# A deadline for background work on TensorE, and measured durations, in a kernel's own list scheduler

## Chip, cores, metric

One core of one Trainium2 chip. The metric is device time in microseconds (us) of one execution. Executions that agree within 1.5% of the fastest count as fast and are compared; the kernel before had one slow one (1389.24 us), which is left out of every ratio.

## The reference

A transformer block on 2048 rows of 640, bf16: layer norm, attention with 32 heads of 20, output projection and residual, layer norm, a gated feed-forward of width 1728, residual.

```python
qkv = x_norm @ wqkv                                    # 2048 x 1920
scores = einsum("bhqd,bhkd->bhqk", q, k) * 20 ** -0.5  # 32 heads of 2048 x 2048
p = softmax(scores); o = einsum("bhqk,bhkd->bhqd", p, v)
h = x + o @ wo
h2 = h + (gelu(norm(h) @ w_gate) * (norm(h) @ w_up)) @ w_down
```

## The kernel before

The queries go through in seven chunks (512, 512, 256, 256, 256, 128, 128 rows), cut into 32 slots. Scores stand in tiles of 128 keys by 512 columns. A *unit* is three or two such tiles: TensorE computes them (QK), ScalarE turns them into exponentials (P) in one instruction of 1536 or 1024 columns. Eight tiles a slot (two in the first) are computed on VectorE instead, by integer arithmetic. TensorE then multiplies P by V (PV). Projections, the feed-forward of the chunk before, and layer norms fill the gaps.

The order of every engine's instructions comes from a list scheduler inside the kernel. It gives each operation a price (`dur`), simulates the engines, and emits what it chose. On the chip each engine runs its list in that order and waits on semaphores, so a wrong price costs nothing by itself; it only leads to another order.

QK is row-tiled, PV column-tiled, all else uses the full array. An exponential waits for two things: its scores (QK), and that the PV which reads the old content of its P tiles is done.

Of the kernel before, what the change touches and what calls it, by code (L numbers as in the profile page):

```python
# [16 lines left out]
DRAIN = {"pe": 0.165, "act": 0.115, "dve": 0.085, "pool": 0.05, "sp": 0.0}  # L17
WARM_WIN, WARM_MIN = 3.4, 0.5
PAD_WIN, PAD_MIN = 3.4, 0.42
PE_AGE = 1.5  # L20

MODE_SWITCH = {"pe": 0.105, "act": 1.28}


class Bank:
# [16 lines left out]
class Sched:  # L42
# [43 lines left out]
    def schedule(self):  # L86
        ops = self.ops
        for o in ops:
            o.nd = len(o.deps)
            for d in o.deps:  # L90
                ops[d].succ.append(o.i)
        free_at = [0.0] * 8
        owner = [None] * 8
        last = [None] * 8
        ready = {e: [] for e in ENGINES}
        future = {e: [] for e in ENGINES}
        free = {e: 0.0 for e in ENGINES}
        mode = {e: None for e in ENGINES}
        for o in ops:
            if o.nd == 0:  # L100
                heapq.heappush(ready[o.eng], (o.prio, o.i))
        events = [0.0]
        done = 0
        order = []
        t = 0.0
        recent = collections.deque()
        live = False
        total = len(ops)
        while done < total:
            assert events, "no operation can start"  # L110
            t = heapq.heappop(events)
            while events and events[0] <= t + 1e-9:
                heapq.heappop(events)
            for e in ENGINES:
                while future[e] and future[e][0][0] <= t + 1e-9:
                    _, p, i = heapq.heappop(future[e])
                    heapq.heappush(ready[e], (p, i))
                if free[e] > t + 1e-9:
                    continue
                skipped = []  # L120
                kept = set()
                chosen = None
                while ready[e]:
                    p, i = heapq.heappop(ready[e])
                    o = ops[i]
                    got = []
                    for bk in o.acq:
                        for b in bk.allowed:
                            if owner[b] is None and free_at[b] <= t + 1e-9 and b not in got and b not in kept:
                                got.append(b)  # L130
                                break
                        else:
                            got = None
                            break
                    if got is None:

                        if p[0] == 0:
                            kept.update(bk.allowed[0] for bk in o.acq)
                        skipped.append((p, i))
                        continue  # L140
                    skipped.append((p, i))
                    if chosen is None:
                        chosen, banks = o, got
                        if e != "pe" or p[0] < 1 or o.mode == mode[e] or t - o.ready > PE_AGE:
                            break
                    elif o.mode == mode[e]:
                        chosen, banks = o, got
                        break
                    if len(skipped) >= 60:
                        break  # L150
                for s in skipped:
                    if chosen is None or s[1] != chosen.i:
                        heapq.heappush(ready[e], s)
                if chosen is not None:
                    for bk, b in zip(chosen.acq, banks):
                        bk.b = b
                        owner[b] = bk
                        if last[b] is not None:
                            chosen.deps = set(chosen.deps)
                            chosen.deps.add(last[b])  # L160
                if chosen is None:
                    if e == "pe" and self.warm is not None:
                        while recent and recent[0][0] < t - WARM_WIN:
                            recent.popleft()
                        b = self.warm_bank
                        free7 = (owner[b] is None and free_at[b] <= t + 1e-9
                                 and all(hasattr(ops[d], "fin") and ops[d].fin + 0.06 <= t for d in self.warm_deps))
                        if sum(x for _, x in recent) < WARM_MIN * WARM_WIN and (free7 or live):
                            o = Op()
                            o.i, o.eng, o.lat = len(ops), "pe", DRAIN["pe"]  # L170
                            o.prio, o.sem, o.tag, o.util = (9, 0), None, "warm", 0.213
                            o.acq, o.rel, o.succ, o.dur = [], [], [], 0.215
                            if live and (mode[e] == "col" or not free7):
                                o.fns, o.mode, o.deps = list(self.pad), "col", set()
                            else:
                                o.fns, o.mode = [self.warm], "full"
                                o.deps = set(self.warm_deps) | ({last[b]} if last[b] is not None else set())
                                last[b] = o.i
                            ops.append(o)
                            chosen = o  # L180
                            total += 1
                    if chosen is None:
                        continue
                o = chosen
                if e == "pe" and self.pad is not None and o.tag and o.tag[0] == "O":
                    while recent and recent[0][0] < t - PAD_WIN:
                        recent.popleft()
                    u = sum(x for _, x in recent) + o.util
                    while u < PAD_MIN * PAD_WIN and o.util < 1.1:
                        o.fns = o.fns + self.pad  # L190
                        o.dur += 0.215
                        o.util += 0.213
                        u += 0.213
                    live = o.i not in self.final
                o.start = t
                if o.util:
                    recent.append((t, o.util))
                if o.mode is not None:
                    if mode[e] not in (None, o.mode):
                        o.dur += MODE_SWITCH[e]  # L200
                    mode[e] = o.mode
                free[e] = t + o.dur
                o.fin = t + o.dur + o.lat
                heapq.heappush(events, free[e])
                for bk in o.rel:
                    b = bk.b
                    owner[b] = None
                    free_at[b] = o.fin + SEM_LAT.get((e, "pe"), SEM_ANY)
                    last[b] = o.i
                    heapq.heappush(events, free_at[b])  # L210
                for s in o.succ:
                    q = ops[s]
                    q.ready = max(q.ready, free[e] if q.eng == e == "pe" else o.fin + SEM_LAT.get((e, q.eng), SEM_ANY))
                    q.nd -= 1
                    if q.nd == 0:
                        heapq.heappush(future[q.eng], (q.ready, q.prio, q.i))
                        heapq.heappush(events, q.ready)
                order.append(o)
                done += 1
        self.order = order  # L220
        self.span = max(o.fin for o in ops)
# [93 lines left out]
P_QK, P_PV, P_PRO, P_EPI, P_LN, P_BG = 0, 1, 1.5, 2, 2.5, 3  # L315


def bass_sequential_preLN__mha_block__glu_gated_geglu__prompt_kernel(
# [12 lines left out]
    with ExitStack() as es:  # L331
# [8 lines left out]


        def c_mm(n, passes=1):
            return 0.001 + passes * n / 2400.0

        def c_act(n):
            return 0.052 + n * 0.000833
# [6 lines left out]
        identf = sb("identf", [128, 128], FP32)  # L353
# [19 lines left out]
        osb = sb("osb", [128, 2, 512], FP32)  # L373
# [75 lines left out]
        def cst(fn, key, n=128):  # L449
# [7 lines left out]
           reads=["zer"], writes=["qf1"])  # L457
        op("act", I("activation", f32(qt_all[:, 2, :, :]), zer[:, 0:2].bitcast(FP32).to_broadcast([128, 2048]), ACT.Copy), 1.8, P_QK,
           reads=["zer"], writes=["qf2"])
# [295 lines left out]
        for c, (q0, nq) in enumerate(CHUNKS):  # L755
            n = 512 // nq
# [11 lines left out]
        i, in_slot = 0, {}  # L768
# [178 lines left out]
        def epilogue(s_, bk):  # L947
# [13 lines left out]
            for tt in range(4):  # L961
                op("pe", lambda eng, tt=tt: eng.transpose(bank(b2)[:, tt * 128:(tt + 1) * 128],
                                                          osb[:, s, tt * 128:(tt + 1) * 128], identf[:]),
                   c_mm(128, 4), P_EPI, mode="full", reads=[("osb", s), "identf"], writes=[key], acq=[b2] if tt == 0 else [],
                   after=tuple(aft) if tt == 0 else ())
            bv = lambda: bank(b2).rearrange("p (t j e) -> p t j e", t=4, j=4)
            rcv = rc[:, s, :].rearrange("p (t j) -> p t j", t=4)
# [220 lines left out]
```

## Time and profile before

| | us |
|---|---|
| time, median of the fast runs | 927 to 929 |
| span of the profile | 925.5 |
| up to the first exponential / from first to last / after the last | 35.7 / 853.7 / 36.1 |
| stalls of ScalarE between exponentials, summed | 12.9 |

A *stall* here is what the distance from one exponential's start to the next exceeds the undisturbed 1.331 us (1536 columns) or 0.904 us (1024). I sort those over 0.06 us into two kinds: if a QK matmul started 0.33 to 0.48 us before the delayed exponential, it waited for scores (*late QK*); if none did, its own scores were ready earlier and it waited for P tiles (*P-slot*). The *tail* is what comes after the last exponential.

### The profile page before, as it was taken

How to read it: one execution, taken by the hardware profiler on the slowest of the kernel's cores; microseconds unless marked ns; L12 is line 12 of the kernel's file. 1: busy time of each engine (PE TensorE's matmuls, PEld its weight loads, DVE VectorE, ACT ScalarE, POOL GpSimd, SP SyncE). 2: the span in 40 equal slices, each digit the busy share in tenths (PEclk: the TensorE clock that was granted, in tenths of full speed). 3: DMA queues.
4: the chain of work that ended last, by engine and by line, in shares of the span. 5: the costliest groups of instructions: out<-in, count | busy, mean ns of one | idle time of the engine just before them, and what ended most of it. 6: DMA issues, size and time to landing. Idle time of an engine off the chain costs nothing.

```text
span 925.5 us, 23154 instructions
## 1 busy us (share of the span) xinstructions
PE 845.3 (91%) x10109; PEld 354.8 (38%) x10109; DVE 810.3 (88%) x1703; ACT 885.7 (96%) x801; POOL 35.1 (4%) x117
## 2 busy tenths in 40 slices
PE   3998999999998998999888999999989999999998
PEld 2432322222232222233233333344444445555667
DVE  8859999999898998888798997989998997998873
ACT  6899999999999999999999999999999999999962
POOL 5000000000001000000001000001000000000100
DMA  7301010322550000001021000010100000110000
GB/s 256 95 18 44 18 55 18 90 60 66 152 180 16 15 1 1 1 15 44 1 31 23 9 2 1 16 30 10 37 16 16 9 23 2 31 32 10 10 17 16
DMA packets 39517, 34.36 MB, mean 37 GB/s; under 512 B 19436, under 2 KB 36936, under 8 KB 39416
## 3 DMA queue, kind: packets, MB, share of 16 engines
q1 hardware_dynamic: 39416, 32.89, 12.7%
q8 instruction: 79, 1.29, 0.6%
q14 instruction: 22, 0.18, 0.1%
HBM read 20.12 MB, written 8.09 MB: 30 GB/s over the span
## 4 chain that ended last, share of the span: by engine, by line
ACT 72%; PE 14%; DVE 11%; issue 1%; POOL 0%; DMA 0%
ACT pts L339 46%; ACT rege L339 25%; PE ps L1039 4%; DVE qt_all L339 3%; PE ps L616 3%; PE ps L852 3%; PE ps L339 3%; DVE rege L339 2%; PE ps L1096 2%; DVE qt_all L812 1%; DVE rege L812 1%; DVE stats L339 1%; ACT L339 1%; DVE rege L1074 1%; PE ps L561 0%
## 5 line engine op out<-in xcount | busy, mean ns | idle before, releaser
L339 ACT ACTIVATE pts<-ps 128x1536 bf16<-128x1536 f32 x480 | 573.1, 1379 | 4.9 <-PE ps L852 3.7
L852 PE MATMUL ps<-qt_all,kt_all 32*128 32x256 bf16 (+2 forms) x3584 | 303.4, 289 | 43.2 <-ACT pts L339 27.5
L339 ACT ACTIVATE rege<-ps 128x1536 bf16<-128x1536 f32 x239 | 300.1, 1381 | 2.1 <-PE ps L339 1.5
L852 PEld LDWEIGHTS ps<-qt_all,kt_all 32*128 32x128 bf16 x3584 | 95.0, 92 | 276.8 <-ACT pts L339 160.8
L339 DVE TENSOR_TENSOR qt_all<-qt_all 128x1024 bf16<-128x1024 bf16 (+1 forms) x240 | 164.0, 683 | 3.4
L1039 PE MATMUL ps<-rege,regw 128*128 128x256 bf16 (+2 forms) x980 | 154.7, 290 | 9.9 <-ACT rege L339 4.2
L339 PE MATMUL ps<-pts,v_all 128*21 128x256 bf16 (+2 forms) x2098 | 138.8, 290 | 0.5 <-DVE rege L339 0.5
L812 DVE TENSOR_SCALAR rege<-ps 128x512 int16<-128x512 f32 x154 | 105.3, 685 | 27.6 <-PE ps L852 26.8
L339 DVE TENSOR_SCALAR qt_all<-qt_all 128x1024 bf16<-128x1024 int16 (+1 forms) x288 | 115.8, 417 | 2.5
L339 PE MATMUL ps<-rege,v_all 128*21 128x256 bf16 (+2 forms) x1294 | 113.3, 292 | 0.1
L1039 PEld LDWEIGHTS ps<-rege,regw 128*128 128x128 bf16 x980 | 72.5, 98 | 67.9 <-issue 28.5
L616 PE MATMUL ps<-regw 128*128 128x512 bf16 (+1 forms) x360 | 86.9, 351 | 1.9 <-DVE v_all L749 0.7
L1096 PE MATMUL ps<-regw,rege 128*128 128x320 bf16 x448 | 79.4, 301 | 1.1 <-DVE rege L1064 0.5
L812 DVE TENSOR_SCALAR qt_all<-ps 128x512 int16<-128x512 f32 x96 | 65.6, 684 | 3.7 <-PE ps L852 2.6
L339 DVE TENSOR_SCALAR rege<-rege 128x1024 int16<-128x1024 int16 (+2 forms) x166 | 67.1, 421 | 1.3
L339 DVE TENSOR_TENSOR rege<-rege 128x1024 bf16<-128x1024 bf16 (+3 forms) x103 | 65.5, 644 | 0.9
L339 PEld LDWEIGHTS ps<-pts,v_all 128*21 128x21 bf16 x2098 | 50.2, 91 | 37.2 <-issue 31.6
L339 PE MATMUL ps<-kt_all,zer 128*32 128x512 bf16 x676 | 56.6, 384 | 0.0
L1096 PEld LDWEIGHTS ps<-regw,rege 128*128 128x128 bf16 x448 | 36.7, 97 | 32.4 <-issue 15.8
L339 PEld LDWEIGHTS ps<-rege,v_all 128*21 128x21 bf16 x1294 | 41.0, 91 | 20.6 <-issue 14.3
L1085 DVE TENSOR_TENSOR rege<-rege,ps 128x512 bf16<-128x512 bf16 (+1 forms) x53 | 35.7, 676 | 12.1 <-PE ps L1039 11.8
L616 PEld LDWEIGHTS ps<-regw 128*128 128x128 bf16 x360 | 28.6, 98 | 45.2 <-issue 21.0
(95 smaller groups left out, 574.3 us busy)
## 6 DMA issues: line engine op xcount, KB each, us to landing
rege<-in_A_x_dram SPq DMA_DIRECT2D x6, 640.0 KB, 5.1
q_rows<-regw SPq DMA_DIRECT2D x20, 128.0 KB, 1.7
out_dram<-rege SPq DMA_DIRECT2D x16, 160.0 KB, 2.1
regw<-in_B_w_gate_dram SPq DMA_DIRECT2D x1, 2160.0 KB, 11.9
regw<-in_B_w_up_dram SPq DMA_DIRECT2D x1, 2160.0 KB, 16.9
regw<-in_B_w_down_dram SPq DMA_DIRECT2D x1, 2080.0 KB, 22.9
kt_all<-k_rows SPq DMA_DIRECT2D x12, 160.0 KB
qt_all<-q_rows SPq DMA_DIRECT2D x12, 160.0 KB
```

The costliest lines, as they stand in the source:

```text
L339: return lambda eng: getattr(eng, method)(*args, **kwargs)
L616: yield op("pe", lambda eng, l=l, r=r, k=k: eng.matmul(bank(bk, n), l, r, start=(k == 0), stop=(k == len(steps) - 1)), c_mm(n), prio, mode ...
L812: d_ops.append(op("dve", lambda eng: eng.tensor_scalar(v[:, 512 * h:512 * h + 512], bank(b), EXP_MUL, -32000.0, ALU.mult, ALU.max), c_dve( ...
L852: return lambda eng: eng.matmul(out()[:, kk * nq:(kk + 1) * nq], kt_all[32 * j:32 * j + 32, g, kt * 128:(kt + 1) * 128], qt_all[32 * j:32 ...
L1039: op("pe", lambda eng, a=a, f=f, fi=fi: eng.matmul(bank(bk)[:, fi * nq:(fi + 1) * nq], w[:, a, F0[f]:F0[f] + 128], hnT[:, a, 128 * tb:128 ...
L1074: cp.append(op("dve", lambda eng, bg=bg, fv=fv, w=w: eng.tensor_copy(fv, bank(bg, w)), c_dve(w), p, reads=[kg], writes=hkeys(k), rel=[bg], ...
L1085: hdone.append(op("dve", lambda eng, bu=bu, fv=fv, w=w: eng.tensor_tensor(fv, fv, bank(bu, w), ALU.mult), c_dve(w), p, reads=[ku] + hkeys( ...
L1096: op("pe", lambda eng, f=f, o=o, hf=hf, bk=bk: eng.matmul(bank(bk, 320), ha_f[:, o:o + 128], wd[:, f, hf * 320:(hf + 1) * 320], start=(f = ...
```

## The change

The intent: TensorE should not start background work, a PV or padding that would still run when the next QK has to start; and the scheduler's prices for TensorE should be the measured ones.

```diff
+QK_LEAD = .45
-MODE_SWITCH = {"pe": 0.105, "act": 1.28}
+MODE_SWITCH = {"pe": .098, "act": 1.28}
+        due = None
...
+                    if e == "pe" and due is not None and o.prio[0] > 0 and t < due < t + o.dur + (MODE_SWITCH[e] if mode[e] not in (None, o.mode) else 0):
+                        skipped.append((p, i))
+                        if len(skipped) >= 60:
+                            break
+                        continue
...
-                    while u < PAD_MIN * PAD_WIN and o.util < 1.1:
+                    room = due - t - MODE_SWITCH[e] if due is not None and due > t else 1e9
+                    while u < PAD_MIN * PAD_WIN and o.util < 1.1 and o.dur + 0.215 < room:
...
+                if e == "act":
+                    due = t + o.dur + (0.905 if o.dur > 1.2 else 1.332) - QK_LEAD if o.mode == "exp" else None
...
-            return 0.001 + passes * n / 2400.0
+            return 0.004 + passes * n / 2400.0
...
-                   c_mm(128, 4), P_EPI, ...      # the epilogue's fp32 transposes
+                   c_mm(128, 2.5), P_EPI, ...
```

I call the first block the *gate*, the second the *cap*, the rest the *prices*.

More of the change, by code (lines that the diff above doesn't have):

```diff
@@ L963, in epilogue @@
                                                           osb[:, s, tt * 128:(tt + 1) * 128], identf[:]),
-                   c_mm(128, 4), P_EPI, mode="full", reads=[("osb", s), "identf"], writes=[key], acq=[b2] if tt == 0 else [],
+                   c_mm(128, 2.5), P_EPI, mode="full", reads=[("osb", s), "identf"], writes=[key], acq=[b2] if tt == 0 else [],
                    after=tuple(aft) if tt == 0 else ())
```

## The prediction

> **What bounds the kernel now.** I read the page's first part, then busy time by stage, ScalarE's waits, the timeline of ScalarE, and at the end the tail. The page's first line and the table by stage (us; the stages are before the first exponential, first to last exponential, after the last):
>
> ```profile
> PE 845.3 (91%) x10109; PEld 354.8 (38%) x10109; DVE 810.3 (88%) x1703; ACT 885.7 (96%) x801; POOL 35.1 (4%) x117
> ```
> ```profile
> 0.00:35.67 35.67, 21.14 (x154) 12.28 (x154) 30.25 (x97) 24.58 (x45) 12.12 (x32) 1.00 0.55 186
> 35.67:889.40 853.73, 793.37 (x9530) 316.93 (x9530) 765.76 (x1573) 850.12 (x743) 23.00 (x85) 1.00 0.12 32
> 889.40:925.50 36.10, 30.74 (x428) 25.56 (x426) 14.34 (x35) 11.02 (x14) 0.00 (x0) 1.00 0.04 15
> ```
>
> In the middle stage ScalarE is busy 850.1 of 853.7 us. TensorE's 793.4 is inflated, since matmuls overlap in the trace. The next question is how much of ScalarE's time is avoidable. Its timeline (start us, us, instruction, count, idle before it):
>
> ```profile
> 42.41 4.67 ACT L339 ACTIVATE pts<-ps 128x1536 bf16<-128x1536 f32 x4
> 46.88 2.46 ACT L339 ACTIVATE rege<-ps 128x1536 bf16<-128x1536 f32 x2
> 49.11 4.74 ACT L339 ACTIVATE pts<-ps 128x1536 bf16<-128x1536 f32 x4
> ...
> 92.84 2.37 ACT L339 ACTIVATE pts<-ps 128x1536 bf16<-128x1536 f32 x2 [0.57 <-PE ps L339]
> ```
>
> From 42.41 to 49.11 six exponentials take 6.70 us, so a pair (1536 columns, then 1024) costs 2.235 us at the bare rate. Start to start, the trace's instructions give 1.331 and 0.904 us as the undisturbed values. I summed over all exponentials what the distance to the next exceeds these by: 12.9 us in all, 10.0 of it in 41 stalls over 0.06 us. No single view prints this sum; busy time hides it because a long record overlaps its neighbour. The middle stage is thus 802.4 bare + 12.9 stalls + 36.9 for five excursions to Gelu with their table loads + 1.6 for the last exponential = 853.8. **12.9 us, 1.4% of the span, is all that a perfect QK service could save in this stage.**
>
> What a stall waits for, from ScalarE's waits (us in total, times, longest):
>
> ```profile
> ACT pts L339 <- PE ps L852: 3.7, 1, 3.7
> ...
> ACT rege L339 <- PE ps L339: 1.5, 1, 1.5
> ...
> ACT pts L339 <- PE ps L339: 0.9, 2, 0.6
> ...
> ACT rege L339 <- PE ps L852: 0.7, 2, 0.4
> ```
>
> The first is the start of the stream, before any exponential. L852 is QK. L339 on ps is PV (or its padding): there an exponential waits not for scores but for the PV that still reads the P slot it will overwrite. The three largest stalls (1.57, 0.86 and 0.50 us, at 144, 93 and 196 us) end together with a long PV at the close of a slot; 2.9 of the 12.9 us. Of the rest nearly all are before a 1536-wide exponential after a 1024-wide one, with QK late by 0.06 to 0.6 us.
>
> The tail of 36.1 us is the other term that can move. Its TensorE is busy 30.7 us, and work of the last-but-one query chunk reaches into it:
>
> ```profile
> 900.49 1.70 ACT L339 ACTIVATE rege<-rege 128x1792 bf16<-128x1792 bf16 x1 [2.86 <-DVE rege L1074]
> 902.21 1.28 ACT L339 ACT_TABLE_LOAD   x1
> ```
>
> 1792 columns are 14 blocks of 128, the Gelu of a whole 128-row chunk; the very last chunk's Gelu is done in pieces on qt_all. So chunk 5's feed-forward is a backlog that TensorE had not finished when the exponentials ended.
>
> **What the Trainium skill says.** "ScalarE: Activation LUTs", What happens when an exp ACTIVATE runs: 0.833 ns per element whatever the function. The trace agrees: (1.331 - 0.904) / 512 = 0.834 ns, so nothing here makes an exponential itself cheaper. "TensorE: Matmul & The Clock Gate", Back-to-back issue gap: N/2.4 + 2.5 ns warm. Medians start to start here are 216, 135.5, 109 and 55.5 ns for N = 512, 320, 256, 128, so N/2.4 plus 2 to 3; the new constant of 4 ns is nearer than the old of 1. "TensorEngine Tiling (Array Packing)", Key Properties: changing the tiling mode drains the engine. A row-tiled QK of 512 columns followed by column-tiled PV takes 315 ns against 216, so 99 ns; the new 98 is right and the old 105 too long. "TensorE: Matmul & The Clock Gate", Part 1: the clock is halved after an idle window of about 3.4 us. Every window of this profile shows clock 1.00, so the padding is enough here; the 1389 us run among the three of the kernel before may be such a throttled one, which its times alone can't show.
>
> **The change, part by part.** The program does the same arithmetic: all this code sits in the list scheduler that fixes each engine's order of instructions. Only the order, and the number of padding matmuls (676 in 169 groups of four) and warming ones (55), can change.
>
> 1. Durations in the scheduler. Mode switch 0.105 to 0.098: I count 1586 switches among row, column and full mode in the trace, so 11.1 us less. Matmul constant 1 to 4 ns: 980 + 520 + 448 + 23 = 1971 matmuls priced so, 5.9 us more. Epilogue transposes from 0.214 to 0.137 us: 128 of them, 9.9 us less. Measured, two of these fp32 transposes start 109 or 164 ns apart, mean 144, so the new price is right. Sum: 15 us less TensorE time in the plan, 1.7% of the 854 us. The hardware doesn't get faster; the plan puts background work a little earlier and denser. I estimate 1 to 2 us from this: fewer mismatches in the middle, somewhat less backlog in the tail.
>
> 2. The gate. At the start t of an exponential, due is set to t + 1.332 + 0.905 - 0.45 = t + 1.787, for both widths. That is the latest start for the QK of the second unit on, which reuses this exponential's banks. But at the start of the next exponential due is overwritten, 0.455 us (after 1536) or 0.882 us (after 1024) before it falls due. So a background operation is stopped only if it starts during the exponential and lasts beyond that. A full-mode matmul takes at most 0.217 + 0.098 = 0.315 us, and is never stopped. An unpadded PV with a switch takes 0.436 + 0.098 = 0.534, and is stopped only in the last 0.08 us of a 1536-wide one; long or padded PVs in the last half microsecond. Laying the rule over the trace before, 11 of 333 column-mode runs would have been held. The gap between the overwrite and the banks' release (0.171 us) is unguarded, although a PV started there delays QK by up to 0.25 us. At 11 holds with 0.1 to 0.3 us each, the gate can save 1 to 3 us; a held PV that is released right after the overwrite can also lose as much. I take 1 us of gain.
>
> 3. The cap on padding. A pad group is 0.215 us and is added only while the PV ends before due. Only 17 of the 343 runs I count have three or more groups; a handful will lose one or two. I take 0 to 1 us.
>
> Sum: 12.9 us of stalls fall to some 10, the tail shrinks by 1, so 929.3 - 4 = 925. It is small because what the gate guards is seldom violated.
>
> **The rivals.** (a) Holding PV back keeps the P slots full longer, and the exponential then waits for PV instead of QK. The three largest stalls already have this form; but PV mostly starts right after a QK, 0.4 us into an exponential, where nothing is held. If it did bite at every slot's close (32 slots, 0.3 us), +10 us: 939. (b) TensorE has too little slack and the gate throws some away: idle gaps ahead of QK push the feed-forward back and lengthen the tail. For it: chunk 5's Gelu already sits in the tail. Against it: 48 us of padding and warming (224 times 0.216) plus roughly 100 us of idle (the start-to-start distances beyond N/2.4, 3 ns and a switch, summed) are still there. It would make 930 to 940. (c) The opposite: the denser plan completes chunk 5 before the stream ends, and its TensorE work (140 matmuls at 55.5 ns and 28 at 135.5, 11.6 us) leaves the tail in part: 915 to 920. (d) Less padding lets the clock fall for a window or more: some microseconds a time; if for good, a time like the 1389 us one. (e) The reordering is chaotic: one changed choice shifts everything after it, and 41 stalls are redrawn. I put this noise at +-5 us, which is more than the intended effect.
>
> **Range and chances.** 925, with 914 to 936 eight times in ten: noise and the tail. Over 2% faster means under 910.7, more than all the stalls plus a third of the tail's excess; 2 in 100. Over 2% slower, above 947.9, takes rival (d), or (a) and (b) together: 6 in 100.
>
> **What would show it.** Counts of QK, PV, projection and feed-forward matmuls the same, pads between 560 and 720. Bare exponentials still 1.331 and 0.904 us, 719 of them. Summed stalls 6 to 14 us. First exponential within 0.5 us of 35.67. Tail 31 to 39 us. Clock 1.00. The prediction is wrong if the stalls fall under 4 us (then the gate does much more than the durations above allow), if the tail moves by over 6 us, or if the granted clock falls.

## More of the kernel before

The parts that matter here:

```python
SIZES = (512, 512, 256, 256, 256, 128, 128); PR, PR2 = 12, 6   # 18 P tiles in a ring
D_PER_SLOT = (8,) * len(SIZES)                                  # tiles a slot for VectorE
P_QK, P_PV, P_PRO, P_EPI, P_LN, P_BG = 0, 1, 1.5, 2, 2.5, 3     # lower goes first
...
def schedule(self):
    ...
                while ready[e]:
                    p, i = heapq.heappop(ready[e])
                    o = ops[i]
                    ...                              # are its PSUM banks free?
                    skipped.append((p, i))
                    if chosen is None:
                        chosen, banks = o, got
                        if e != "pe" or p[0] < 1 or o.mode == mode[e] or t - o.ready > PE_AGE:
                            break
                    elif o.mode == mode[e]:          # prefers the tiling mode TensorE is in
                        chosen, banks = o, got
                        break
    ...
                if e == "pe" and self.pad is not None and o.tag and o.tag[0] == "O":   # a PV
                    ...
                    while u < PAD_MIN * PAD_WIN and o.util < 1.1:
                        o.fns = o.fns + self.pad     # four matmuls with zeros keep the clock up
                        o.dur += 0.215
...
# a unit's QK, the QK of a VectorE tile, and a PV of so many quads
qk = op("pe", fns, 0.215, P_QK, mode="row", ...)
qd = op("pe", [...], 0.08, P_QK + 0.5, mode="row", writes=[("SD", xd)], after=[qk])
pv = op("pe", fns, 0.218 * len(quads), P_PV, mode="col", reads=reads, writes=[("O", s_), "pvseq"], acq=acq)
# the PV that closes a slot also takes all VectorE tiles that are left
while final and d_done: ...; quads.append(have)
```

Before: 6.8 us late QK in 37 stalls, 3.3 us P-slot in 4.

## The result

926.83 us (median of 4), against 928.55 for the kernel before (with its slow run; 927.77 is the median of its three fast ones). The ratio is 0.9987 with a 95% interval of 0.9967 to 1.0006: the same. (A ratio here is the mean time of one kernel's fast runs over that of the other's of the same rounds, so not quite the ratio of the medians.) The output is correct.

The changed kernel's first line of the page, and busy time by stage (before the first exponential, first to last, after the last). Its spans show that little changed in sum and more in the parts:

```profile
PE 836.7 (91%) x10152; PEld 358.4 (39%) x10207; DVE 810.1 (88%) x1703; ACT 886.3 (96%) x801; POOL 35.8 (4%) x117
```
```profile
0.00:35.17 35.17, 20.44 (x152) 12.19 (x154) 30.25 (x97) 24.58 (x45) 12.12 (x32) 1.00 0.56 188
35.17:892.07 856.90, 790.48 (x9632) 324.31 (x9684) 765.61 (x1573) 850.66 (x743) 23.69 (x85) 1.00 0.12 32
892.07:924.24 32.17, 25.77 (x373) 21.87 (x370) 14.24 (x34) 11.02 (x14) 0.00 (x0) 1.00 0.05 17
```

The middle stage is 3.2 us *longer*, the tail 3.9 us shorter, the start 0.5 shorter: -1.3. In the middle ScalarE does the same work (850.7 busy); the stalls grew from 12.9 to 15.9 us: late QK from 6.8 to 7.8, P-slot from 3.3 to 5.8.

ScalarE's waits of the changed kernel (us in total, times, longest) beside those of before in the prediction. QK is now L862, helpers L349. The waits for PV (PE ps L349) grew:

```profile
ACT pts L349 <- PE ps L862: 4.2, 3, 3.7
ACT pts L349 <- PE ps L349: 3.9, 3, 1.8
...
ACT rege L349 <- PE ps L862: 0.7, 2, 0.6
...
ACT rege L349 <- PE ps L349: 0.2, 1, 0.2
```

The largest of them in the changed kernel's timeline (start, us, instruction, count, idle before it). The QK group that holds the waiting unit's scores starts at 593.90 and is done by 594.5. But the exponential starts only at 595.49, with the end of the PV that closes the slot; VectorE's copy of that PV's result starts a tenth later:

```profile
593.90 0.57 PE L862 MATMUL ps<-qt_all,kt_all 32*128 32x256 bf16 x8
594.39 0.50 PE L349 MATMUL ps<-pts,v_all 128*21 128x256 bf16 x10
...
594.84 0.39 PE L349 MATMUL ps<-qt_all,v_all 128*21 128x256 bf16 x4
595.06 0.39 PE L349 MATMUL ps<-rege,v_all 128*21 128x256 bf16 x4
595.38 0.85 PE L1106 MATMUL ps<-regw,rege 128*128 128x320 bf16 x5
595.49 1.02 ACT L349 ACTIVATE pts<-ps 128x1024 bf16<-128x1024 f32 x1 [1.80 <-PE ps L349]
595.57 0.68 DVE L349 COPY osb<-ps 128x512 f32<-128x512 f32 x1
```

The rows with qt_all and with the last rege are VectorE tiles. The closing PV is one operation, so P tiles that ScalarE filled long ago stay locked until VectorE has delivered its own.

The tail: the Gelu of chunk 5 starts 3.2 us after the last exponential (892.07) instead of 11.1 (900.49 against 889.40), and the output is done sooner:

```profile
892.08 1.28 ACT L349 ACT_TABLE_LOAD   x1
...
895.27 1.70 ACT L349 ACTIVATE rege<-rege 128x1792 bf16<-128x1792 bf16 x1 [0.39 <-DVE rege L1084]
```

Padding, from the groups of before and after, did not fall but grew from 169 to 192 sets of four. In the plans 162 and 190 of these sets are put in where TensorE has nothing else to start, by a part of the scheduler that the cut above leaves out; only 7 and 2 stand in a PV, where the cap could act:

```profile
L339 PE MATMUL ps<-kt_all,zer 128*32 128x512 bf16 x676 | 56.6, 384 | 0.0
```
```profile
L349 PE MATMUL ps<-kt_all,zer 128*32 128x512 bf16 x768 | 63.1, 384 | 0.0
```

**What the plan says of the gate.** I read the scheduler's plan, which is the list of start times that it computes while the program is built, and logged when the gate holds something. It does so at nine moments in the whole program. At four of them it holds a closing PV (slots 2, 20, 25 and 31), for 0.3 to 0.7 us; at five it holds full-mode background work, for 0.15 to 0.5 us. These five are at the first exponential after each of the five excursions to Gelu: due is computed before the table load (1.28 us) is added to that exponential's time, so it falls due while the exponential still runs. The cap never acts: the program without it is the same operation by operation.

### The profile page after: what moved, and what is told of

It is laid out like the page before. It is cut to its first block, busy times and chain, and to the rows that moved or that the text cites. A ratio compares the mean times of both kernels' runs of the same rounds, so it can differ in the third digit from the quotient of the medians.

```text
span 924.2 us, 23302 instructions
## 1 busy us (share of the span) xinstructions
PE 836.7 (91%) x10152; PEld 358.4 (39%) x10207; DVE 810.1 (88%) x1703; ACT 886.3 (96%) x801; POOL 35.8 (4%) x117
## 4 chain that ended last, share of the span: by engine, by line
ACT 67%; PE 19%; DVE 12%; issue 1%; POOL 0%; DVEq 0%
ACT pts L349 43%; ACT rege L349 23%; PE ps L862 5%; PE ps L349 4%; PE ps L1106 4%; DVE rege L349 3%; PE ps L1049 3%; DVE qt_all L349 3%; PE ps L626 2%; DVE rege L822 1%; ACT L349 1%; DVE stats L349 1%; PE ps L571 1%; PE ps L972 0%; DVE qt_all L822 0%
## 5 line engine op out<-in xcount | busy, mean ns | idle before, releaser
L349 ACT ACTIVATE pts<-ps 128x1536 bf16<-128x1536 f32 x480 | 570.1, 1356 | 8.7 <-PE ps L862 4.2
L862 PE MATMUL ps<-qt_all,kt_all 32*128 32x256 bf16 (+2 forms) x3584 | 306.1, 289 | 48.4 <-ACT pts L349 28.5
L349 ACT ACTIVATE rege<-ps 128x1536 bf16<-128x1536 f32 x239 | 297.0, 1355 | 1.0 <-PE ps L862 0.7
L862 PEld LDWEIGHTS ps<-qt_all,kt_all 32*128 32x128 bf16 x3584 | 96.8, 92 | 277.1 <-ACT pts L349 161.5
L349 DVE TENSOR_TENSOR qt_all<-qt_all 128x1024 bf16<-128x1024 bf16 (+1 forms) x240 | 164.4, 685 | 3.8
L1049 PE MATMUL ps<-rege,regw 128*128 128x256 bf16 (+2 forms) x954 | 149.2, 287 | 9.8 <-ACT rege L349 5.8
L349 PE MATMUL ps<-pts,v_all 128*21 128x256 bf16 (+2 forms) x2098 | 138.8, 290 | 0.8 <-DVE rege L349 0.8
L349 DVE TENSOR_SCALAR qt_all<-qt_all 128x1024 bf16<-128x1024 int16 (+1 forms) x288 | 116.0, 418 | 2.1
L349 PE MATMUL ps<-rege,v_all 128*21 128x256 bf16 (+2 forms) x1294 | 113.0, 292 | 0.6 <-DVE rege L349 0.6
L626 PE MATMUL ps<-regw 128*128 128x512 bf16 (+1 forms) x341 | 81.8, 348 | 3.2 <-DVE regw L656 0.9
L349 DVE TENSOR_SCALAR rege<-rege 128x1024 int16<-128x1024 int16 (+2 forms) x166 | 67.5, 422 | 1.3
L349 DVE TENSOR_TENSOR rege<-rege 128x1024 bf16<-128x1024 bf16 (+3 forms) x103 | 65.9, 646 | 0.9
L349 PEld LDWEIGHTS ps<-pts,v_all 128*21 128x21 bf16 x2098 | 50.3, 91 | 37.9 <-issue 30.7
L349 PE MATMUL ps<-kt_all,zer 128*32 128x512 bf16 x768 | 63.1, 384 | 0.0
L1106 PEld LDWEIGHTS ps<-regw,rege 128*128 128x128 bf16 x448 | 36.6, 97 | 33.4 <-issue 15.0
L349 PEld LDWEIGHTS ps<-rege,v_all 128*21 128x21 bf16 x1294 | 40.9, 91 | 20.1 <-issue 14.0
```

The source lines that it names most:

```text
L349: return lambda eng: getattr(eng, method)(*args, **kwargs)
L626: yield op("pe", lambda eng, l=l, r=r, k=k: eng.matmul(bank(bk, n), l, r, start=(k == 0), stop=(k == len(steps) - 1)), c_mm(n), prio, mode ...
L862: return lambda eng: eng.matmul(out()[:, kk * nq:(kk + 1) * nq], kt_all[32 * j:32 * j + 32, g, kt * 128:(kt + 1) * 128], qt_all[32 * j:32 ...
L1049: op("pe", lambda eng, a=a, f=f, fi=fi: eng.matmul(bank(bk)[:, fi * nq:(fi + 1) * nq], w[:, a, F0[f]:F0[f] + 128], hnT[:, a, 128 * tb:128 ...
L1106: op("pe", lambda eng, f=f, o=o, hf=hf, bk=bk: eng.matmul(bank(bk, 320), ha_f[:, o:o + 128], wd[:, f, hf * 320:(hf + 1) * 320], start=(f = ...
```

## The experiments

Theory R: the gate is nearly idle. Any edit redraws a chaotic plan, and the time is decided by where the draw puts the closing PVs (P-slot stalls) and how much of chunk 5 is left for the tail. Theory G: the gate protects QK as intended and the prices make the plan better because they are truer.

All results in one table. Ratios are to the kernel before, run on the same chip in the same rounds. Stalls and tail are of the profiled run, in us; "stalls" is the net sum with the many small ones.

| run | median us | ratio (95%) | stalls | P-slot | late QK | tail |
|---|---|---|---|---|---|---|
| before | 927.77 | 1 | 12.9 | 3.3 | 6.8 | 36.1 |
| after | 926.83 | 0.9987 (0.9967 to 1.0006) | 15.9 | 5.8 | 7.8 | 32.2 |
| e1 prices only | 929.73 | 1.0020 (1.0007 to 1.0032) | 18.0 | 5.4 | 9.7 | 34.0 |
| e2 gate only | 932.18 | 1.0050 (1.0037 to 1.0064) | 18.3 | 7.7 | 8.0 | 36.1 |
| e3 gate not on PV | 929.10 | 1.0019 (1.0005 to 1.0033) | 18.0 | 7.5 | 8.0 | 32.2 |
| e4 closing PV in two | 927.32 | 0.9997 (0.9985 to 1.0010) | 12.2 | 2.3 | 6.7 | 36.2 |
| e5 switch 0.097 | 937.69 | 1.0103 (1.0084 to 1.0123) | 24.6 | 11.3 | 10.9 | 36.6 |
| e6 due kept | 933.20 | 1.0061 (1.0047 to 1.0075) | 21.5 | 11.6 | 7.6 | 32.4 |
| e7 old transpose price | 932.90 | 1.0056 (1.0043 to 1.0070) | 17.8 | 8.1 | 7.3 | 36.2 |
| e8 split, six tiles | 923.20 | 0.9950 (0.9938 to 0.9963) | 12.2 | 0.7 | 8.5 | 30.7 |
| e9 QK prices | 934.29 | 1.0066 (1.0052 to 1.0080) | 17.4 | 8.8 | 6.5 | 37.5 |
| e10 = e8 + e9's prices | 924.14 | 0.9960 (0.9946 to 0.9974) | 11.5 | 0 | 8.7 | 30.8 |
| e11 = e10, no gate | 921.21 | 0.9930 (0.9917 to 0.9944) | 9.6 | 0 | 6.7 | 30.2 |
| e12 six tiles only | 925.69 | 0.9979 (0.9965 to 0.9993) | 14.9 | 4.4 | 7.8 | 30.3 |

All outputs were correct, and every run of e1 to e12 is of the fast state. The differences below rest on the 95% intervals.

One correction belongs to the table. The profiled runs of e1, e2 and e5 hold stretches at half clock of 3.413 us each (two in e1), and the record's granted clock shows such runs in most kernels: 1.000 without a stretch, 0.998 or 0.996 with. On the three chips of e1 to e12 the kernel before took 929.21, 929.76 and 929.76 us in its 0.998 runs and 926.5 to 928.3 in the others, so a stretch cost that kernel some 2 us, as much as the change is worth. The stalls in and just after these stretches count as late QK in the table: 2.6 us of e1's 9.7, 1.2 of e2's 8.0 and 2.9 of e5's 10.9. Without them late QK is 6.5 to 8.7 us in all fourteen kernels.

### e1, e2: the two halves

```diff
# e1: the changed kernel, gate and cap off
-if e == "pe" and due is not None and o.prio[0] > 0 and t < due < ...
+if False and due is not None and t < due < ...
-while u < PAD_MIN * PAD_WIN and o.util < 1.1 and o.dur + 0.215 < room:
+while u < PAD_MIN * PAD_WIN and o.util < 1.1:
# e2: the changed kernel with 0.105, 0.001 and c_mm(128, 4) as before
```

> The three new durations, without the gate and without the cap on padding. Theory R (the prices redraw the plan and shorten the tail; the gate's few holds fall on the PV that closes a slot and turn into waits for P slots): the three stalls of the changed kernel at 595, 729 and 883 us (2.04, 0.46 and 1.35 us) are gone or under 0.4 us, but another large one may be drawn; the tail is 33 to 35 us, that is 1.5 to 3 us shorter than before; time 926 to 929. Theory G (the gate does what it is meant for): without it the summed stalls are larger than the 15.9 us of the changed kernel, mostly QK that comes late, and the time is that of the kernel before or worse.

> The gate and the cap with the old durations. Theory R: no saving; large waits for P slots at the close of some slots, summed stalls 15 to 19 us, the tail still 36 to 38 us, time 930 to 934. Theory G: summed stalls below the 12.9 us of the kernel before, time 924 to 928.

e1 was 929.73, a little above my range. Of the three stalls of the changed kernel that I named, two are gone and the first is 0.56 us instead of 2.04; others were drawn (2.16 us at 170, 1.12 at 813). Part of its loss is neither theory's: the profile of e1 has two stretches of 3.413 us in which the clock record says half speed, at 465.6 and 858.1 us. Four stalls there sum to 2.6 us (1.41, 0.48, 0.20, 0.51). Busy time of e1 in windows of 3.4 us (the columns are stretch, length, then busy time of TensorE, its weight loads, VectorE, ScalarE, GpSimd, then granted clock):

```profile
461.40:464.80 3.40, 2.45 (x49) 0.89 (x42) 3.30 (x7) 3.40 (x5) 0.00 (x0) 1.00 0.83 50
464.80:468.20 3.40, 3.01 (x27) 1.24 (x27) 2.16 (x6) 2.27 (x3) 0.00 (x0) 0.61 0.67 133
```

Without those stalls e1's sum is 15.4 us, against 15.9 with the gate. So in this pair the gate changed the stalls by next to nothing; e1's late QK without the four is 7.1, against 7.8. Its tail, which comes after the second slow stretch, is 34.0 instead of 32.2. One of e1's five runs took 927.72 with a granted clock of 1.000, the other four 929.6 to 929.9 with 0.996 to 0.998. So e1's one run at full clock lies 0.9 us above the changed kernel's median.

e2 was 932.18 with stalls of 18.3 us and the old tail, as R had it; G wanted fewer than 12.9. The gate on the old prices left late QK where it was (6.8 us without the stalls of the slow stretch) and made P-slot stalls 4.5 us worse. So the two halves alone are +0.2% and +0.5%, and together -0.1%. The parts don't add, which is what a redraw looks like.

### e3: do the held PVs make the P-slot stalls?

```diff
-... o.prio[0] > 0 and t < due < ...
+... o.prio[0] > 1 and t < due < ...     # PV (priority 1) is never held
```

> The whole change, but the gate holds only operations of lower priority than PV. Theory R: the P-slot stalls at the close of slots 20, 25 and 31 should go if the hold itself makes them, and stay if the PV is late for another reason (the preference for the mode that TensorE is in comes first in the scheduler); the kernel's own plan still shows them at 591, 722 and 874 us, so I expect two or three of them to stay, and a further one of some 2 us near 168 us that the hold had removed by chance; time 928 to 931. Theory G: the PV holds are part of what protects QK, so QK stalls grow by 1 us or more in many small pieces.

All three named stalls stayed (2.03, 0.46 and 1.35 us), so the hold doesn't cause them: my first idea, that a held PV turns into a P-slot stall, fell here. A new one of 2.16 us stands at 172 us, where the changed kernel has one of 0.37. The small stalls from late QK didn't grow as G expected (8.0 against 7.8).

### e4: take the lock away

```diff
-for have in quads: ...                          # one PV, 0.218 * len(quads)
+for part in ([quads[:n_first], quads[n_first:]] if len(quads) > n_first else [quads]):
+    ...                                         # ScalarE's quads, then VectorE's
```

> The whole change, with the PV that closes a slot issued in two parts: the quads whose P tiles ScalarE wrote, then the quads of the tiles that VectorE computes. The P slots come free with the first part. Theory R: the summed stalls fall from 15.9 to 8 to 12 us, those over 0.4 us to at most two; but the background work loses TensorE and VectorE time to the faster stream, so the tail grows to 36 to 39 us and the time stays 926 to 930. Rival (the large stalls come from late QK and not from P slots): the summed stalls stay at 14 to 17.

With the closing PV in two parts the P-slot stalls fell from 5.8 to 2.3 us, in one place instead of six, and the stalls in sum from 15.9 to 12.2. The sum is just above the 8 to 12 that I gave. This edit redraws the plan as any other does, so one run would be weak evidence for the P tiles; but all four kernels with the split (e4, e8, e10, e11) have P-slot stalls of 2.3 us or less, and all ten without it 3.3 or more. In ScalarE's waits of e4 one entry for PV is left:

```profile
ACT rege L349 <- PE ps L349: 2.2, 1, 2.2
```

But the time stayed at 927.32, since the tail went back to 36.2 us. In its trace chunk 5's Gelu starts 11.2 us after the last exponential. What the middle won, the tail took. My reading is that when the stream of exponentials ends earlier, less background work has been done by then; no run tests this alone.

### e5: one nanosecond

```diff
-MODE_SWITCH = {"pe": .098, "act": 1.28}
+MODE_SWITCH = {"pe": .097, "act": 1.28}
```

> The whole change with 0.097 us in place of 0.098 for a mode switch: one nanosecond, less than the trace can tell (it shows 96 to 99). Theory R (each time is one draw of a chaotic plan; the constants of the change are a lucky one): several us slower although the price is as true; the kernel's own plan has 12 us more, so 933 to 940, with P-slot stalls of 10 us or more, the largest near 198 us, and a tail of 37 to 39 us. Rival (better prices make a better plan, and the time follows from their truth): within 1 us of the changed kernel, 926 to 928.

937.69 us, 10.9 above the changed kernel, for a price that is as true: the trace shows 95 to 101 ns for a switch after 512 columns. Two of its four runs have a slow stretch; the two at full clock took 936.3, still 9.5 above. The largest difference is at the close of slot 5:

```profile
195.84 0.83 PE L349 MATMUL ps<-kt_all,zer 128*32 128x512 bf16 x12
...
196.69 2.33 PE L626 MATMUL ps<-regw 128*128 128x512 bf16 x10
...
198.95 0.60 PE L349 MATMUL ps<-pts,v_all 128*21 128x512 bf16 x6
...
200.04 1.02 ACT L349 ACTIVATE pts<-ps 128x1024 bf16<-128x1024 f32 x1 [4.58 <-PE ps L349]
```

TensorE pads, because its next PV waits for VectorE's tiles (in the plan ScalarE's part is ready at 190.9, VectorE's at 195.4). Then ten projection matmuls go first, since TensorE is in full mode and the scheduler prefers the mode it is in for up to 1.5 us; the closing PV starts at 198.95. ScalarE stands still for 4.6 us. A step in price that the trace can't resolve thus moves the time by more than the change did: the change's time rests on the draw.

### e6: the gate as it was probably meant

```diff
+dues = collections.deque()        # a due time stays until its QK has been issued
-due = t + o.dur + (0.905 if o.dur > 1.2 else 1.332) - QK_LEAD if o.mode == "exp" else None
+if o.mode == "exp":
+    dues.append(t + o.dur + (0.905 if o.dur > 1.2 else 1.332) - QK_LEAD)
+else:
+    dues.clear()
+due = dues[0] if dues else None
+# and when TensorE issues a unit's QK: dues.popleft(); due = dues[0] if dues else None
```

> The whole change, but every QK's due time is kept in a list until that QK has been issued, so it isn't overwritten 0.455 or 0.882 us before it falls due. If the overwriting is why the gate does little against late QK: the stalls from late QK fall from 7.8 us to 5 to 6.5. If these come from the chip running a little behind the plan, which the gate can't see: they stay at 7 to 8.5. In both cases the redraw costs: the plan shows a wait of almost 5 us for P slots near 196 us, so P-slot stalls 9 to 12 us and a time of 930 to 935.

With the deadline no longer overwritten, late QK is 7.6 instead of 7.8 us. That is outside the 5 to 6.5 expected if the overwriting were the reason, and within the 6.5 to 8.7 of the other draws. So mending the overwriting, which is real, brought no gain clear of a redraw; that the chip runs a little behind the plan fits this, but isn't shown. The rest is redraw again (4.75 us of P-slot stall at 199.5).

### e7: which price gave the shorter tail?

```diff
-c_mm(128, 2.5)
+c_mm(128, 4)
```

> The whole change with the old price of the epilogue's transposes (0.214 us instead of 0.137). Theory R: the shorter tail comes above all from this price, since the plan with it has the old tail; so tail 36 to 38 us, and with redrawn P-slot stalls 932 to 938. Rival (the tail comes from the gate or the switch price): tail 32 to 34 us.

Tail 36.2, time 932.90: as expected. But e4 and e5 have the new price and the old tail too. So the tail doesn't follow from this price. With eight VectorE tiles in the last chunk it is near 32, or at 36 to 37.5, with chunk 5's Gelu some 3 us or some 11 to 13 us after the last exponential; only e1, at 34.0 and 8.3 us, lies between. In e7's timeline:

```profile
894.92 1.28 ACT L349 ACT_TABLE_LOAD   x1
...
906.07 1.70 ACT L349 ACTIVATE rege<-rege 128x1792 bf16<-128x1792 bf16 x1 [2.64 <-DVE rege L1084]
```

### e8, e12: the backlog of the last chunk

```diff
# e8: the split of e4, and
-if e != "pe" or p[0] < 1 or o.mode == mode[e] or t - o.ready > PE_AGE:
+if e != "pe" or p[0] <= 1 or o.mode == mode[e] or t - o.ready > PE_AGE:   # PV needn't wait for its mode
-D_PER_SLOT = (8,) * len(SIZES)
+D_PER_SLOT = (8,) * (len(SIZES) - 1) + (6,)
# e12: the changed kernel with the D_PER_SLOT line alone
```

> An attempt to beat both: the change, the closing PV in two parts, PV taken ahead of work in the same mode, and in the last 128-row chunk 6 instead of 8 exponential tiles a slot on VectorE. If P slots and the backlog of the last chunks are what is left to gain: summed stalls 9 to 12 us, P-slot stalls under 2.5 us, tail 30 to 33 us although the stream ends earlier, time 921 to 924, faster than both kernels. If the two terms only trade with each other, 926 to 928.

> The change with nothing but 6 instead of 8 VectorE tiles a slot in the last chunk, to tell e8's parts apart. The order is the same up to the last two slots. The tail is a backlog of VectorE and TensorE: with 4 tiles fewer for VectorE it shrinks by 1.5 to 3 us, the 1.35 us stall near 883 goes, and ScalarE gets 4 tiles more (4 times 0.427 = 1.7 us); 924.5 to 926.

e12: the tail fell from 32.2 to 30.3 us, the stall near 883 went, and the time is 925.69. So the tail is in part a backlog of VectorE. e8: P-slot stalls 0.7, tail 30.7, time 923.20, under both kernels by 0.4 to 0.5%. Its sum of stalls, 12.2, is just above the 9 to 12 expected. What taking PV ahead of its mode adds to the split was not run alone.

### e9, e10: does late QK come from the price of QK?

The trace gave two prices that the change had left wrong. Laying the plan's list over the weight loads of the changed kernel (10207 in both, in the same order), the distance from a unit's QK to the next operation in another mode is 0.324 us without and 0.325 with a one-matmul QK of a VectorE tile right behind it (0.339 with two matmuls). So that tile's QK, on the fourth row group, costs almost nothing there, in 199 of 250 cases. In the other 51 no unit's QK is just before it. In 31 of these another mode follows, and it takes 0.218 us (0.317 to 0.325 with the switch); in 20 another QK follows, 0.01 to 0.60 us after it. The plan has 0.08 for all. One that stands alone, between feed-forward matmuls, takes from 654.68 to 655.00:

```profile
654.47 0.28 PE L1049 MATMUL ps<-rege,regw 128*128 128x256 bf16 x1
654.68 0.39 PE L862 MATMUL ps<-qt_all,kt_all 32*128 32x256 bf16 x2
...
655.00 0.28 PE L1049 MATMUL ps<-rege,regw 128*128 128x256 bf16 x1
```

```diff
+if e == "pe" and o.tag and o.tag[0] == "SD":
+    o.dur = 0.01 if last_pe is not None and last_pe.tag and last_pe.tag[0] == "S" else 0.218
-qk = op("pe", fns, 0.215, P_QK, ...)
+qk = op("pe", fns, 0.227, P_QK, ...)
# e9: on the changed kernel.  e10: on e8
```

> The whole change, with two more prices as the trace has them: the QK of a VectorE tile costs next to nothing right after its unit's QK (0.325 us to the next operation, against 0.324 without it; 199 of 250 cases) and 0.218 us alone (51 cases), where the plan takes 0.08 for both; a unit's QK 0.227 instead of 0.215. If late QK comes from the chip running behind a plan with wrong prices: stalls from late QK fall from 7.8 to 3 to 5.5 us. Rival (they come from semaphores, or from VectorE): they stay at 7 or more. In both cases the redraw decides the rest: the plan has P-slot waits of some 8 us and a long tail, so 930 to 936.

> Run e8 with the two QK prices of e9, the gate in. If the prices make QK punctual: late-QK stalls 4 to 6 us instead of e8's 8.5, P-slot stalls under 1, time 919.5 to 922. If they do nothing: 923.

A miss. Late QK went from 7.8 to 6.5 in e9, between the two bands that I had set, and from 8.5 to 8.7 in e10, where I expected 4 to 6. 924.14 is no better than e8. Prices nearer to the trace for QK alone don't make QK punctual (0.218 is still too much in most of the 20 cases in which a QK follows); whatever else makes it late stays open.

### e11: what the gate is worth without P-slot stalls

```diff
# e10 with the gate and the cap off, as in e1
```

> e10 without the gate and the cap. With P-slot stalls out of the way this asks what the gate itself is worth. Theory R (nothing, or a loss; every difference is a redraw): within 3 us of e10 on either side, late-QK stalls within 1 us of e10's; the plan is 1.7 us shorter, so 918 to 921. Theory G: late-QK stalls 2 us or more above e10's.

921.21 us, 0.7% under the kernel before, 0.6% under the changed one, and the fastest of all. Both e10 and e11 have no P-slot stall, so here late QK can be compared without them: 8.7 us with the gate, 6.7 without. That is outside R's band (within 1 us of e10's), on the side opposite to G. The start, the middle and the tail are all a little shorter than e10's (36.3, 854.2 and 30.8 us):

```profile
0.00:36.02 36.02, 21.47 (x154) 12.36 (x154) 30.25 (x97) 24.58 (x44) 12.12 (x32) 1.00 0.55 184
36.02:888.49 852.47, 802.02 (x9735) 325.66 (x9734) 759.25 (x1560) 851.81 (x745) 24.84 (x85) 1.00 0.12 32
888.49:918.74 30.25, 23.89 (x344) 20.00 (x342) 11.58 (x30) 10.91 (x15) 0.00 (x0) 0.99 0.04 13
```

I don't conclude that the gate costs 3 us. A difference of this size is within what a redraw does, and a third of it is the clock: three of e10's five runs have slow stretches, and at full clock it took 922.5 and 923.3, e11 920.8 to 921.2. What can be said is the sign pattern: the gate's addition moved the ratio from 1.0020 to 0.9987 (after against e1, where a slow clock explains some of it), from 1 to 1.0050 (e2 against before), and from 0.9930 to 0.9960 (e10 against e11). In none of the three pairs did it lower late QK: 7.1 to 7.8, 6.8 to 6.8, 6.7 to 8.7 (e1 and e2 without their slow stretches).

## Why the prediction was right, and where its steps were wrong

**The time** was right: 925 with 914 to 936 predicted, 926.8 measured, and "within 2%" had 92 in 100. The bound that carried it held: 12.9 us of stalls are all that QK service could give, so no large gain was to be had. That it came within 2 us of 925 is luck: the sum starts from 929.3, a median of three runs with the slow one among them, the stalls missed their term by 5.9 us in one direction, the tail by 2.9 in the other. Of the steps only the gate's idleness was right, and that in part.

- **"12.9 us of stalls fall to some 10": wrong in sign.** They rose to 15.9. The steps that failed are the 1 us of gain from the gate, which assumed that holds save late QK, and the fewer mismatches expected of the prices. Late QK rose by 1.0 us and P-slot stalls by 2.5. Range given 6 to 14.
- **"the tail shrinks by 1": mis-sized.** It shrank by 3.9, which is what made the changed kernel no slower. The mechanism, less backlog of chunk 5, is right (Gelu 3.2 instead of 11.1 us after the last exponential); this is rival (c)'s effect, but its 915 to 920 didn't come, since the stalls rose. That it follows from the denser plan is not shown, since e4 and e5 have nearly the same prices and a tail of 36 us. The whole -1.3 us of the profiled span is -3.9 (tail) - 0.5 (start) + 3.2 (middle).
- **The gate's idleness: right**, and so was the reason for part of it, the overwritten due. The count of 11 holds, made from the trace before, compares with nine moments in the plan after. But "A full-mode matmul ... is never stopped" was wrong: at five of these moments full-mode work was stopped, because at the first exponential after a Gelu the table load keeps due in force past its 0.905 or 1.332 us. And closing the unguarded gap which I named moved late QK by 0.2 us (e6), less than the draws differ.
- **The cap: "a handful will lose one or two" was wrong.** None did. I had taken the padding in the trace for padding in PVs, but in the plan before only 7 of the 169 groups, in 4 PVs, are that; the rest fills idle time and the cap doesn't touch it. Pads rose to 768, outside the 560 to 720 that I gave.
- **Rival (a)** named the right wait, P slots at a slot's close, with the wrong cause: not the holding of PV (e3), but that the closing PV is one operation and waits for VectorE's tiles (e4), and that the scheduler prefers other work in the present mode (e5).
- **Rival (e), chaos, "+-5 us": right in kind, too small.** One nanosecond of one price gave 10.9 us (9.5 at full clock).
- **Rival (d), the clock**, I thought rare. The traces of both kernels show no run of slowed matmuls, but they hold no clock record at all, so my "clock 1.00" rested on nothing recorded. e1, e2 and e5 have one or two stretches of 3.413 us at half clock each.
- **Two readings were wrong.** The third largest stall is not the one of 0.50 us: 0.63 at 534.9 and 0.51 at 514.1 us are larger, and both are late QK. And the medians, 2 to 3 ns over N/2.4, lie about as near to the old constant of 1 ns as to the new one of 4.

**Left open:** what makes QK late, by 6.5 to 8.7 us in sum outside slow stretches, in all fourteen kernels. Mending the overwritten due (e6) and the two QK prices (e9, e10) brought no gain clear of the redraws. The exponentials that wait for it are nearly always 1536 wide after a 1024 wide one, where a QK has 0.284 us between the release of its banks and its due time in the plan (t + 1.332 + 0.171 to t + 1.787).

## What to carry to other kernels

When a static scheduler produces the program, an edit's time is one draw: shift one price by a nanosecond and compare before crediting an effect of under 1%. Look for what makes draws bad, here one operation that holds a buffer ring while it waits for a second producer, and take that away; split, PV ahead of its mode, six tiles and the QK prices with no gate (e11) gave 0.7%, the intended change 0.1%. e11 is one draw too; e8 and e10 without its last step gave 0.5 and 0.4%. The scheduler itself can sort the draws: built again, the fourteen kernels have planned spans of 907.4 (e11) to 925.4 us (e5), and each median lies 10.6 to 15.1 us above its plan; the change's plan is 2.9 us under the one before. Read the plan's span before crediting the idea. And follow a saving to the end of the program: in e4 the stalls fell by 3.7 us and the tail took 4.0.

## What the Trainium skill lacked or had wrong

- "TensorE: Matmul & The Clock Gate", Part 1 and the table Why this matters for your kernels, speak of idle gaps of about 3 us or more as what lowers the clock; the page's section on a second failure mode has frequent short gaps do it too, but gives no busy share at which it happens. In e1 the clock was halved at 465.6 us although TensorE's longest idle gap in the preceding 3.41 us was 0.95 us, and it was busy for 2.14 us of them; in the other three stretches the longest gap before was 1.03 to 2.21 us. The length of a slow stretch, 3.413 us, and the half clock agree with the page in all four that were recorded (two in e1, one each in e2 and e5).
- "TensorEngine Tiling (Array Packing)", Key Properties, says that a change of mode drains the engine, but not what it costs: 95 to 101 ns here (from a QK of 512 columns to the full-mode or PV matmul after it 315 to 317 ns, from a PV to a QK 311, against 216 without a change).
- "TensorE: Matmul & The Clock Gate", Part 4, gives bf16 transposes (about 390 ns in isolation, about 275 ns in one kernel) and none in fp32. Here, in a row, fp32 transposes of 128 columns start 109 or 164 ns apart, 144 on average in the kernel before.
- No page says that a PSUM or SBUF ring can be held by an operation that waits for another producer; in e4, which splits that operation, P-slot stalls fell from 5.8 to 2.3 us.
